# Last chunk's key-value products joined in held PSUM banks, two residuals added on TensorE, six spare matmuls taken out, and a new order table

## The chip, the cores and the metric

The kernel runs on one core of one Trainium2 chip. The metric is the device time of one execution, in microseconds (us); lower is better. A core has TensorE (PE, with its weight loads PEld), VectorE (DVE), ScalarE (ACT), GpSimd (POOL) and SyncE (SP), which here only issues DMAs. PSUM is used as four double banks of 128 x 1024 float32 (the program's D0 to D3, "D" in the profile).

## The reference

Two attention layers A and two linear layers B alternate on x of 2048 tokens by 512, bfloat16, 32 heads of 16. Cut to what matters here:

```python
x = A_x
x = x + _A_ref(_layernorm(x), A_wq, A_wk, A_wv, A_wo, A_beta)
x = x + _B_ref(_layernorm(x), B_wqkv, B_w_phi, B_wo)
x = x + _A_ref(_layernorm(x), ...)
x = x + _B_ref(_layernorm(x), ...)

# _B_ref
phi_k = concatenate([softmax(pk), softmax(-pk)], -1)      # pk = k @ w_phi, per head
kv = einsum('bhsf,bhsd->bhfd', phi_k, v)                  # sum over all 2048 tokens
z = einsum('bhsf->bhf', phi_k)
num = einsum('bhqf,bhfd->bhqd', phi_q, kv)
den = einsum('bhqf,bhf->bhq', phi_q, z)[..., None] + 1e-06
return (num / den) ... @ wo
```

Layer A works on four segments of 512 tokens: causal attention inside the segment, plus a read from a memory that the earlier segments have filled. Layer B needs its kv and z over all tokens before the first query can be answered, so every B layer has one turning point: the end of the keys.

## The kernel before

The sixteen tiles of 128 tokens are held in SBUF as `X`. A small graph (`Graph.op`) records every operation with what it reads and writes; `Graph.place` (L172) then takes three things from a compressed table, `ORDER`: the sequence of all operations, the engine of each, and the buffer of each tile. `Graph.emit` (L205) writes one instruction stream per engine in that sequence and puts semaphore waits where an engine needs another's result or a buffer that another still uses. Each engine runs its stream strictly in the table's order, and SP its DMAs too. No planner runs in the kernel: where the table puts an operation is where it runs.

The helpers name most lines of the profile. `mm` (L334, matmuls at L341) and `pair` (L345, matmuls at L356) issue matmuls on 64 rows of the array, so that two run side by side; `pair` issues two halves, and its second half waits for its first (`hard=o1`). `act` is L366, `evac` copies out of PSUM at L374 (ACT) or L375 (DVE), `tr` is a DMA transpose from SP (L383), `dma` a plain one (L387).

For each segment s of a layer: the A attention of its four tiles (`a_att`, in two halves), the output projection `out_proj` (L905), whose result is added to `X` by DVE (`res`, L926), the layer norm (L590 to L619), and the B keys of the chunk (`b_keys`, L950). Tiles 14 and 15 are projected one at a time (`SOLO`), the others in pairs. `b_keys` makes, for the tiles of a "part", the key projection (BK), two exponentials on ACT, their sums on DVE (`Zred`, L985), reciprocals (`rZ`, L405), the value projection (BV), its scaling by the reciprocals (`Vt`, L1007), and then the key-value products (KV): for each of two groups q of the feature blocks, one `pair` into a double bank of its own, which `kv_add` (L930) adds into `KV32` in SBUF (`KVacc`, L937 for the first, L939 for the others). Chunks 0 to 2 are one part of four tiles; chunk 3 is two parts, `((0, 1, 2), (3,))`: three tiles, then the last tile alone. After the last of them come the masked copies `Rkv` (L943) and `Rz` (L946), which the queries read.

`b_query` (L1029) makes the query projections (BQ) and their exponentials on ACT, the denominators on PE (`Zq`, L1049, from `Rz`) with a chain of small ACT and DVE steps after them (L1058 to L1068), then for each tile the numerators (`N`, L1076, from `Rkv`), a product (`nmul`, L1087 or L1090), the sum of two halves (`nadd`, L1093, on DVE or POOL by the table), a DMA transpose (`otr`), the projection, the add into `X` and, in the second layer, the store.

At the end of the program `keep` (L671) adds six pairs of 64 x 512 matmuls on a constant, whose result nobody reads; the table puts them in the last 35 us.

## Time and profile before

| | |
|---|---|
| median of 3 runs | 463.37 us (462.33 to 463.4) |
| the profiled execution | 462.93 us, of which 461.2 us are the span from the first to the last instruction |
| mean granted TensorE clock | 0.998 |
| busy share of the span | PE 95%, ACT 91%, DVE 90%, POOL 17% |

One execution was profiled. The rows name the line of the helper, the engine, the operation and its operands by the program's names. Matmuls overlap, so the start of one row to the start of the next tells more than the length of a row: eight 64 x 512 matmuls read as 1.04 us, and the next row begins 0.87 us after they did.

### The profile page before, as it was taken

What the parts mean: (1) busy time and instruction counts of PE and PEld (TensorE: products, weight loads), DVE (VectorE), ACT (ScalarE), POOL (GpSimd) and SP (SyncE); (2) the same over time, 40 slices, a digit from 0 to 9 for tenths busy, and PEclk for the clock granted to TensorE, in tenths of its full rate; (3) what the DMA queues carried; (4) which work ended last, traced back from release to release, by engine and by line L of the source; (5) the groups of instructions that cost most, each with busy time, mean ns of one, the idle gap of its engine ahead of it and who ended that gap; (6) DMA issues with size and microseconds to landing.
All of it is one profiled execution on the core that took longest, in us unless ns stands there. A gap on an engine that the chain in (4) does not pass through costs nothing.

```text
span 461.2 us, 25354 instructions
## 1 busy us (share of the span) xinstructions
PE 437.7 (95%) x11716; PEld 295.6 (64%) x11716; DVE 416.2 (90%) x807; ACT 420.3 (91%) x542; POOL 80.1 (17%) x160
## 2 busy tenths in 40 slices
PE   8989899899999999998899999999999999998896
PEld 4456667667776776675456677677677677666553
DVE  6989998898889999898999899998899889998896
ACT  4999999899999998789699999999999999878991
POOL 2402021101221211102532031130221023110020
PEclk9999999999999999999999999999999999999999
DMA  8554642552233322100243443264113321200357
GB/s 247 127 150 80 127 63 37 75 96 54 50 46 54 46 40 36 37 3 4 48 54 78 71 85 72 49 96 61 26 39 49 50 39 27 48 14 1 50 121 180
DMA packets 90058, 30.37 MB, mean 66 GB/s; under 512 B 76640, under 2 KB 89952, under 8 KB 89952
## 3 DMA queue, kind: packets, MB, share of 16 engines
q1 hardware_dynamic: 89520, 28.48, 33.3%
q8 instruction: 92, 1.51, 1.4%
q10 hardware_dynamic: 432, 0.27, 0.2%
q14 instruction: 14, 0.11, 0.1%
HBM read 6.32 MB, written 2.10 MB: 18 GB/s over the span
## 4 chain that ended last, share of the span: by engine, by line
PE 48%; ACT 40%; DVE 6%; DMA 3%; issue 2%; SPq 0%
PE D L356 31%; ACT p L366 21%; PE D L341 15%; ACT pF L366 13%; ACT pE L366 5%; DMA p<-p 2%; PE D L662 2%; DVE X L926 1%; DMA X<-in_A_x_dram 1%; DVE p L1090 1%; DVE p L375 1%; DVE stats L590 1%; ACT pS L366 1%; DVE p L611 0%; DVE pK L375 0%
## 5 line engine op out<-in xcount | busy, mean ns | idle before, releaser
L366 ACT ACTIVATE p<-D 128x1024 bf16<-128x1024 f32 (+2 forms) x224 | 216.0, 1004 | 13.5 <-PE D L356 9.7
L366 ACT ACTIVATE pF<-D 128x896 bf16<-128x896 f32 x128 | 116.7, 940 | 2.8 <-PE D L341 2.5
L341 PE MATMUL D<-pK,pQ 64*128 64x256 bf16 (+3 forms) x1536 | 112.9, 243 | 4.1 <-ACT pF L366 1.0
L341 PEld LDWEIGHTS D<-pK,pQ 64*128 64x128 bf16 x1536 | 55.2, 94 | 40.7 <-ACT pF L366 5.4
L341 PE MATMUL D<-pV,pF 64*128 64x34 bf16 x1024 | 73.8, 175 | 0.4 <-ACT p L366 0.4
L341 PE MATMUL D<-pW,pF 64*128 64x34 bf16 x1024 | 71.3, 175 | 0.0
L341 PEld LDWEIGHTS D<-pV,pF 64*128 64x128 bf16 x1024 | 55.3, 93 | 2.3 <-ACT p L366 0.7
L341 PE MATMUL D<-pV,p 64*128 64x34 bf16 x1024 | 53.3, 176 | 0.3 <-issue 0.2
L366 ACT ACTIVATE pE<-D 128x768 bf16<-128x768 f32 x64 | 52.3, 831 | 1.4 <-PE D L341 1.0
L341 PEld LDWEIGHTS D<-pW,pF 64*128 64x128 bf16 x1024 | 51.9, 93 | 0.9
L341 PE MATMUL D<-pW,p 64*128 64x34 bf16 x1024 | 52.1, 176 | 0.0
L598 POOL TENSOR_SCALAR rstd<-mv 128x1 f32<-128x1 f32 x60 | 16.1, 272 | 205.9 <-DVE mv L591 205.5
L341 PEld LDWEIGHTS D<-pV,p 64*128 64x128 bf16 x1024 | 47.0, 93 | 3.3 <-issue 0.9
L341 PE MATMUL D<-tri,two 64*128 64x128 bf16 (+1 forms) x384 | 46.7, 234 | 0.4 <-issue 0.4
L341 PEld LDWEIGHTS D<-pW,p 64*128 64x128 bf16 x1024 | 45.2, 93 | 1.3
L590 DVE BATCH_NORM_STATS2 stats<-X 128x6 f32<-128x512 bf16 x64 | 42.9, 680 | 3.0 <-DMA X<-in_A_x_dram 2.5
L341 PE MATMUL D<-pV,pE 64*128 64x34 bf16 x512 | 44.9, 175 | 0.4 <-issue 0.4
L926 DVE TENSOR_TENSOR X<-X,D 128x1024 bf16<-128x1024 bf16 (+1 forms) x36 | 39.4, 1095 | 5.7 <-PE D L356 5.0
L341 PE MATMUL D<-pW,pE 64*128 64x34 bf16 x512 | 42.5, 175 | 0.1
L985 DVE TENSOR_REDUCE pS<-p 128x64 f32<-128x1024 bf16 (+1 forms) x36 | 38.8, 1088 | 1.8 <-ACT p L366 1.8
L375 DVE CAST p<-D 128x512 bf16<-128x512 f32 x48 | 31.1, 683 | 6.3 <-PE D L356 6.1
L356 PE MATMUL D<-WB_o,p 64*128 64x512 bf16 (+1 forms) x288 | 33.0, 353 | 2.7 <-issue 1.3
(115 smaller groups left out, 988.9 us busy)
## 6 DMA issues: line engine op xcount, KB each, us to landing
pW<-pV SPq DMA_DIRECT2D x16, 136.0 KB, 3.1
out_dram<-X SPq DMA_DIRECT2D x7, 256.0 KB, 2.8
X<-in_A_x_dram SPq DMA_DIRECT2D x3, 512.0 KB, 6.1
pX<-in_B_wqkv_dram SPq DMA_DIRECT2D x3, 512.0 KB, 4.6
p<-p SPq DMA_TRANSPOSE x76, 2.8
pX<-p SPq DMA_TRANSPOSE x54, 3.2
WA_k<-in_A_wk_dram SPq DMA_DIRECT2D x2, 256.0 KB, 6.3
WA_q<-in_A_wq_dram SPq DMA_DIRECT2D x2, 256.0 KB, 7.0
```

The source lines that it names most:

```text
L341: ins = e.matmul(out_ap, lhsT, rhs, start=st, stop=sp, tile_position=(basep(lhsT), basep(out_ap)))
L356: ins = e.matmul(out_ap, lhsT[64 * hf:64 * hf + 64], rhs[64 * hf:64 * hf + 64], start=k == 0 and i == 0, stop=k == 1 and i == len(lists[hf ...
L366: return self.g.op({"act": (dur, lambda e: e.activation(out_ap(), in_ap(), func, scale=scale))}, reads, writes, opens, label=label)
L375: "dve": ((340 if fast else n / 0.96 + 65), lambda e: e.tensor_copy(out_ap(), in_ap()))}
L590: v(lambda e: e.bn_stats(self.stats[:, t, :], self.X[:, t, :]), 602, [R("X", t)], [R("st", t)], label="bn")
L598: v(lambda e: e.tensor_scalar(rs, self.mv[:, t, 1:2], LN_EPS, None, op0=ALU.add), 170, [R("mv", t)], [R("rstd", t)], eng="pool", label="rstd")
L662: ins = e.matmul(D.t[c0:, r0 * 8:r0 * 8 + n], r[:, c0:], ones(r, n), start=True, stop=True, tile_position=(r0, c0))
L926: self.v(lambda e: e.tensor_tensor(X(), X(), src(), ALU.add), 65 + 512 * n / 0.96, pr + xr, xr, label="res")
L985: fn = lambda e, sgn=sgn, eo=eo, Z=Z, n=n: e.tensor_reduce(Z.t[:, 0:64 * n].rearrange("p (k s h) -> p k s h", k=n, s=2)[:, :, sgn, :], eo( ...
L1090: v(lambda e, N=N, Tm=Tm, w=w, shape=shape: e.tensor_tensor(shape(Tm.t[:]), shape(N.t[:]), w(), ALU.mult), 1131, [N, AB[(0, 0)], AB[(0, 1) ...
```

## The change

Five things, cut from the diff:

```diff
-    def pair(self, items, cols, reads, writes, opens=(), label="", swap=False):
+    def pair(self, items, cols, reads, writes, opens=(), label="", swap=False, begin=True, end=True, prev=None):
...
-    ... start=k == 0 and i == 0, stop=k == 1 and i == len(lists[hf]) - 1,
+    ... start=begin and k == 0 and i == 0, stop=end and k == 1 and i == len(lists[hf]) - 1,
...
-        o1 = self.g.op({"pe": (dur, half(0))}, reads, writes, opens, label=label, rows=64)
+        o1 = self.g.op({"pe": (dur, half(0))}, reads, writes, opens, label=label, rows=64, hard=prev)
...
             for q in range(2):
-                ps = self.T(self.pD, "gen")
-                self.pair(...
+                join = (L, c) in JOIN
+                if not join or part[0] == 0:
+                    held[q] = (self.T(self.pD, "gen"), None)
+                ps, prev = held[q]
+                o2 = self.pair(...
-                    [ps[0]], label="KV")
-                self.kv_add(ps, q, c == 0 and part[0] == 0, c == 3 and part[-1] == 3)
+                    [ps[0]], label="KV", begin=not join or part[0] == 0, end=not join or part[-1] == 3, prev=prev)
+                held[q] = (ps, o2)
+                if not join or part[-1] == 3:
+                    self.kv_add(ps, q, c == 0 and part[0] == 0, c == 3 and part[-1] == 3)
...
-        res_pe = kind == "b" and all((L, t) in RES_PE for t in ts)
+        res_pe = all((kind, L, t) in RES_PE for t in ts)
...
-RES_PE = set()
+RES_PE = {('a', 1, t) for t in range(14, 16)}
+JOIN = {(0, 3), (1, 3)}
+RZ_ACT = set()
...
-        for _ in range(N_KEEP):
-            self.keep()
...
-N_KEEP = 6
```

1. **Join.** In chunk 3 of both layers the products of the last tile go on adding into the double banks that hold the products of the first three; one add into `KV32` per group takes the place of two. Four `KVacc` go, two in each layer. The first matmuls of the last tile wait for the end of the first part's second half in the same bank (`prev`).
2. **Residual.** For tiles 14 and 15 of the second A layer `X` is added by PE: one more block of matmuls, identity times `X`, in the accumulation (`extra` in `tproj`), and the result is then only copied out of PSUM into `X`.
3. **Keep.** The six pairs of matmuls are gone.
4. **A path not taken.** With `RZ_ACT` the reciprocals could be made on ACT; the set is empty, so nothing changes.
5. **New table.** It holds 2738 operations in place of 2748 (four adds and six `keep` fewer). Read operation by operation in the same way as `place` reads it, and compared with the old one: on PE an operation stands 1.0 places from where it stood on average (at most 11), on ACT 0.3, on DVE 5.1, on SP 3.8. 26 operations change engine. The two residual copies go to ACT. Of the sums `nadd` four go from DVE to POOL and one comes back in the first layer's queries, and in the second layer that of tile 4 goes from POOL to DVE; of the sums after the attention (L882) four go to POOL and four come back; the rest are copies out of PSUM that change places between ACT and DVE, one more leaving ACT than coming to it apart from the residuals, and one small fill of a buffer.

Around the turning point of the second layer PE's stream reads as follows (a "2" is the second half; KV16 to KV19 are the pairs of the first part, groups 0 and 1, then those of the last tile; BQ half-pairs are eight 64 x 512 matmuls each):

```text
before: KV16 KV17 KV16-2 KV17-2 BQ8-2 | KV19 BQ12 KV18 KV19-2 BQ12-2 KV18-2 | Zq17 Zq19 Zq18 Zq16
after:  KV16 KV17 KV16-2 KV17-2 BQ8-2 | KV19 KV18 BQ12 KV19-2 KV18-2 BQ12-2 | Zq27 Zq18 Zq17 Zq16
```

Before, the table gave KV19 the double bank of KV16 and KV18 that of KV17; both had to wait for the adds. At the end of SP's stream, the last DMA transpose (`otr` of tile 14) and a store change places. The buffer that this transpose writes is another one too: before, it was the one from which the transpose of tile 13 reads, so that it had to wait for that one to land; after, it is one that was last read by the projection of tiles 4 and 5. The order of the two:

```text
before: otr(tile 13) otr(tile 12) store(tiles 10, 11) otr(tile 14) store ...
after:  otr(tile 13) otr(tile 12) otr(tile 14) store(tiles 10, 11) store ...
```

## The prediction

> **What bounds the kernel now.** I read the page first, then the busy time by stages, then the chain of waits at the end, then the timeline around the edits.

> ```profile
> 100.00:150.00 50.00, 49.00 (x1449) 35.05 (x1446) 44.86 (x83) 49.93 (x61) 8.59 (x15) 1.00 0.29 51
> 150.00:186.00 36.00, 35.27 (x1118) 24.50 (x1115) 33.51 (x56) 33.62 (x44) 5.30 (x10) 1.00 0.29 41
> 250.00:384.00 134.00, 131.91 (x3951) 93.97 (x3945) 122.19 (x241) 132.65 (x164) 22.17 (x44) 1.00 0.34 56
> 384.00:425.00 41.00, 40.14 (x910) 27.60 (x905) 37.77 (x65) 34.99 (x43) 6.95 (x12) 1.00 0.13 25
> 400.00:412.00 12.00, 12.00 (x184) 6.88 (x177) 11.63 (x20) 9.55 (x12) 1.64 (x4) 1.00 0.17 34
> 425.00:440.00 15.00, 12.72 (x428) 8.21 (x430) 13.35 (x33) 14.59 (x26) 0.00 (x0) 1.00 0.35 54
> ```

> Columns: length, then busy time of PE, PEld, DVE, ACT, POOL, the granted clock, DMA. Three regimes. In the attention (100 to 186, 250 to 384) ACT is full: of 220 us it is idle for 0.07 + 2.38 + 1.35 = 3.8. Towards the turning point of a B layer (384 to 425) PE is full and ACT has room. From 425 ACT is full again, until 440; after that the end hangs on DMAs, as the next view shows. All edits but the table lie in the last two regimes.

> ```profile
> 413.06 11.10 PE D L356 x188
> 424.18 0.73 DVE KV L939
> 424.94 0.21 DVE Rz L946
> 425.19 0.98 PE D L341 x64
> ...
> 434.22 0.39 PE D L678 x2
> ...
> 435.80 0.21 PE D L678 x2
> ...
> 453.12 3.71 DMA p<-p
> ...
> 458.21 0.69 DVE X L926
> ```

> This is the chain that ended last: PE's stream to 424.18, one add, one `Rz`, the first `Zq` at 425.19; later two of the spare pairs (L678); at the end one DMA transpose, 3.71 us, the last projection and the last add.

> **Join, second layer.**

> ```profile
> 420.89 1.34 DVE L939 TENSOR_TENSOR KV<-KV,D 128x544 f32<-128x544 f32 x2
> 421.66 0.22 PEld L356 LDWEIGHTS D<-pT,p 64*128 64x128 bf16 x4 [0.21 <-DVE KV L939]
> 421.98 4.60 ACT L366 ACTIVATE p<-D 128x1024 bf16<-128x1024 f32 x5 [0.20 <-PE D L356]
> 422.98 0.55 PEld L356 LDWEIGHTS D<-pX,WB_q 64*128 64x128 bf16 x8
> 423.20 0.72 DVE L939 TENSOR_TENSOR KV<-KV,D 128x544 f32<-128x544 f32 x1 [0.96 <-PE D L356]
> 423.64 0.32 PEld L356 LDWEIGHTS D<-pT,p 64*128 64x128 bf16 x4
> ```

> The adds that go are the two at 420.89, 1.34 us of DVE. They lie under PE's stream; of them only the 0.21 us is on the path that PE waited for the first add to free the bank. The adds of the last tile stay. The half BQ12-2 (422.98) moves behind KV18-2, which so comes 423.64 - 422.98 = 0.66 us earlier, while the other add still ends only some 0.72 us after its products. So the last add starts not at 424.18 but between 423.3 (all of 0.21 + 0.66 saved) and 423.7 (behind the other add), and `Zq` could start 0.4 to 0.9 earlier. But ACT counts too: it works without a gap on five exponentials from 421.98 to 426.58, and the last two need BQ12, which now ends last; it saves only the 0.21. The first `Zq` of the new order also serves another chunk (64 of them in 0.98, so 16 take 0.24). I take -0.3, between +0.3 and -0.9. The new wait (`prev`) is for KV16-2 and KV17-2; behind it stands all of PE, but BQ8-2's eight matmuls lie in between, so it costs nothing; without that cover it would be a stall of the 0.21 kind for each group.

> **Join, first layer.**

> ```profile
> 202.43 1.35 DVE L939 TENSOR_TENSOR KV<-KV,D 128x544 f32<-128x544 f32 x2
> 203.22 0.80 PEld L356 LDWEIGHTS D<-pT,p 64*128 64x128 bf16 x16
> 204.19 1.35 DVE L939 TENSOR_TENSOR KV<-KV,D 128x544 f32<-128x544 f32 x2 [0.41 <-PE D L356]
> ```

> Here PE did not wait for the first adds (the second row has no idle time before it), and DVE itself waited 0.41 for PE before the last ones. Removing 1.35 under cover gives nothing; the new order puts one BQ half between the last two KV halves, which lets the first add start earlier and the second later. -0.2, between +0.3 and -0.4.

> [...] Here the table gave KV16 and KV19, and KV17 and KV18, the same double bank before, so the holding takes no bank that was free, and the sum has no term for it.

> **Residual.**

> ```profile
> 186.03 1.92 PE L356 MATMUL D<-WA_o,p 64*128 64x256 bf16 x32
> 406.60 0.68 DVE L926 TENSOR_TENSOR X<-X,D 128x512 bf16<-128x512 bf16 x1
> L374 ACT ACTIVATE p<-D 128x512 bf16<-128x512 f32 x28 | 15.9, 597 | 6.7 <-PE D L356 4.6 <-PE D L341 1.9
> ```

> The first row is the same pair of projections in the first layer: 32 matmuls in 1.92, so the eight added ones cost 0.48 of PE, in the stage (400 to 412) where PE is full 12.00 of 12. They take 2 x 0.68 from DVE, which is full too (11.63), and give ACT 2 x 0.60 by the nearest row, where it has 2.45 free. PE sets the end of this stage, so I take +0.4; bounds 0.5 (all of PE's) and -0.5 (the layer norm of these tiles, which waits for the result, comes earlier by part of DVE's 1.36).

> **Sums moved to POOL.**

> ```profile
> 225.00:237.00 12.00, 10.74 (x180) 5.42 (x180) 11.90 (x23) 9.19 (x17) 4.27 (x7) 1.00 0.17 35
> 237.00:250.00 13.00, 13.00 (x223) 7.76 (x223) 12.83 (x28) 12.95 (x18) 3.30 (x8) 1.00 0.60 95
> L1093 POOL TENSOR_TENSOR p<-p 128x512 bf16<-128x512 bf16 x10 | 12.3, 1231 | 65.1 <-DVE p L1090 33.2 <-DVE p L1087 31.6 <-DVE nb L605 0.2
> L1093 DVE TENSOR_TENSOR p<-p 128x512 bf16<-128x512 bf16 x16 | 6.8, 422 | 0.1
> ```

> Three net `nadd` leave DVE, 3 x 0.42 = 1.27 us. Up to 237 DVE alone is full, after it all three are: I take half, -0.6. Each moved sum is 0.81 later (1231 - 422 ns) at its transpose, so the bounds are -1.3 and +0.8. The four sums each way after the attention cancel, as do the copies, within ACT's 0.6.

> **Keep.**

> ```profile
> 447.33 0.59 PE L678 MATMUL D<-onesb 64*128 64x512 bf16 x4
> 447.54 2.85 ACT L366 ACTIVATE p<-D 128x1024 bf16<-128x1024 f32 x3 [0.38 <-PE D L341]
> ```

> Two pairs stand in front of the numerators for which ACT waits 0.38; two others are 0.39 + 0.21 of the chain above, but in a stage where ACT is full 14.59 of 15. I take -0.4, bounds 0 and -1.0.

> **The last transpose.**

> ```profile
> 450.86 1.20 SPq L383 DMA_TRANSPOSE p<-p  x1
> 451.17 0.42 DVE L1093 TENSOR_TENSOR p<-p 128x512 bf16<-128x512 bf16 x1
> 452.10 0.58 SPq L387 DMA_DIRECT2D out_dram<-X  x1
> 453.12 1.19 SPq L383 DMA_TRANSPOSE p<-p  x1
> 456.39 1.22 DVE L926 TENSOR_TENSOR X<-X,D 128x1024 bf16<-128x1024 bf16 x1 [0.17 <-PE D L356]
> ```

> Tile 14's sum ends at 451.59, SP is free at 452.06, yet its transpose starts at 453.12, behind a store and with its buffer not yet free. In the new table it is ahead of that store and in another buffer: 1.06 earlier. The store moved behind loses nothing that lasts: stores end the program only after the last add. DVE's add before the last one ends at 457.61, 0.60 before the last starts, so -0.6 is sure to have room and the rest needs DVE to be earlier too, which the two terms above give. -1.0, bounds 0 and -1.5.

> Sum: -0.3 - 0.2 + 0.4 - 0.6 - 0.4 - 1.0 = -2.1. The profiled execution is 462.93, 1.73 more than its span; the median is 0.44 above it, inside the spread of the three runs. Less 2.1 they give 460.8 and 461.3; I take the shift from the median, **461.3**. The terms' bounds, not all at one end, make its own range 460.0 to 462.8.

> **Rivals.** *The joins and the tail are covered (463.1).* PE and ACT are full before and after 425; if only the residual's +0.4 and the spare pairs' -0.4 reach the end and the transpose gains 0.3, nothing measurable is left. For it: DVE's saved adds are not on the chain. Against: the chain's end shows the gap at SP.

> *The new order closes gaps in the attention (459.2).* Of ACT's idle 3.8 us there 2.38 lie in one stage of 36; were that as tight as the other 184, which lose 1.42, it would lose 0.28, and 2.1 would go on top of the forecast's 2.1. PE's stream is only slightly changed, which speaks against much.

> *The new order opens gaps (466).* The place is the attention, where every exponential that starts late is lost time: if a products' block moves ahead of the scores that ACT needs next, ACT waits. The worst stage now loses 2.38 of 36 (6.6%); the other 184 us lose 1.42. At half the worst rate everywhere, 220 x 0.033 = 7.3, which is +3.5 and, with half of the gains, +2.5. It decides the sign once ACT's idle time there grows by more than the 2.1 gained elsewhere, and can be told from no change at 2.1 + 1.4. For it: DVE's order moves 5.1 places on average; against: ACT's 0.3.

> *The clock falls without the spare pairs (466.6).*

> ```profile
> 447.00:459.00 12.00, 9.26 (x152) 4.86 (x146) 10.44 (x15) 3.61 (x5) 0.00 (x0) 1.00 0.67 153
> 459.00:461.20 2.20, 0.00 (x0) 0.00 (x0) 0.00 (x0) 0.00 (x0) 0.00 (x0) 0.63 0.55 190
> ```

> The granted clock is full to 459 and falls as soon as PE has stopped. If PE's gaps, now filled, made it fall to half from 447 on, PE's 9.26 us of work would double and its 2.74 of idle time swallow a part: +6.5; over half of the stretch +3.3. With the middle, 4.9, and the other terms' -1.7 the time would be 466.6. [...]

> **How the numbers follow.** Forecast 0.50, covered 0.17, gaps closed 0.14, gaps opened 0.14, clock 0.05. From no change I can tell 0.3%, 1.4 us: faster is below 461.98, slower above 464.76. The forecast gives 0.40 of its 0.50 to faster, since most of its own range lies below 461.98, and gaps closed all of its 0.14: 0.54. Same: the other 0.10, covered 0.17, and 0.02 of gaps opened: 0.29. Slower: 0.12 + 0.05 = 0.17. The range, 458.2 to 465.2, leaves out the far parts of both order cases and most of the clock's, about 0.04 + 0.09 + 0.04.

> **What would show it.** Right: the first `Zq` of the second layer within 0.5 of 425.2; four adds fewer at L939; PE not waiting there for an add; the last transpose starting within 0.2 us of SP's previous one, and the last add about 1 us after the add before it starts; DVE below full before 237. Wrong: any ACT idle time in the attention off 3.8 by over 1.5, a granted clock under 1 before the last matmul, or a longer PE stretch than 0.5 before 424.

## The result, and the profile after

The changed kernel is slower: 467.53 us median of 4 runs (466.72 to 471.48) against 462.85 of the kernel before beside it, a ratio of 1.0125 (95% interval 1.0094 to 1.0156). On another chip, measured again (the run after_again below), it was 1.0172 (1.0132 to 1.0213). The forecast was 461.3, its range 458.2 to 465.2. One of the twelve executions of the run no_keep below took 1447.48 us; its median does not hang on it.

The busy time by stages of the changed kernel, with the columns of the prediction's first view:

```profile
100.00:150.00 50.00, 49.31 (x1448) 34.91 (x1440) 44.93 (x83) 49.92 (x62) 9.20 (x15) 1.00 0.34 58
150.00:186.00 36.00, 35.03 (x1090) 24.94 (x1086) 33.06 (x56) 33.18 (x43) 3.19 (x8) 1.00 0.25 34
225.00:237.00 12.00, 12.00 (x166) 5.88 (x166) 11.84 (x21) 9.32 (x15) 6.13 (x8) 1.00 0.19 38
237.00:250.00 13.00, 13.00 (x307) 8.50 (x305) 12.84 (x27) 12.90 (x18) 4.68 (x8) 1.00 0.46 74
250.00:384.00 134.00, 129.77 (x3808) 90.63 (x3804) 116.76 (x230) 129.47 (x158) 23.63 (x44) 0.99 0.36 55
400.00:412.00 12.00, 12.00 (x242) 7.78 (x238) 11.55 (x22) 8.48 (x11) 2.83 (x5) 1.00 0.25 36
425.00:440.00 15.00, 12.53 (x372) 7.80 (x368) 11.61 (x28) 13.45 (x23) 0.00 (x0) 0.77 0.26 38
```

In the attention ACT is now idle for 0.08 + 2.82 + 4.53 = 7.43 us, against 3.8. Nearly all of the growth lies between 250 and 384, where before it was 1.35; PE loses too (129.77 busy, before 131.91). And the granted clock is under 1 in two stages in which it had been 1.00.

The same view cut at the places where the clock changed, first of the changed kernel, then of the kernel before around its turning point:

```profile
314.82:318.23 3.41, 2.56 (x159) 2.38 (x152) 2.86 (x6) 2.71 (x5) 0.00 (x0) 1.00 0.40 70
318.23:321.65 3.42, 3.42 (x25) 1.30 (x22) 1.52 (x2) 2.65 (x3) 0.00 (x0) 0.50 1.10 105
427.46:430.87 3.41, 2.69 (x176) 2.37 (x168) 1.53 (x4) 3.35 (x9) 0.00 (x0) 1.00 0.02 5
430.87:437.70 6.83, 5.85 (x132) 3.65 (x134) 6.61 (x17) 5.86 (x11) 0.00 (x0) 0.50 0.39 61
```

```profile
425.44:428.86 3.42, 2.83 (x186) 2.52 (x179) 1.81 (x5) 3.33 (x9) 0.00 (x0) 1.00 0.02 5
428.86:432.27 3.41, 2.94 (x110) 1.94 (x111) 3.41 (x10) 3.41 (x8) 0.00 (x0) 1.00 0.15 31
```

The clock is halved for one stretch of 3.41 us in the attention and for two of them after 430.87, each time after a stretch in which PE was busy for 2.56 and 2.69 of 3.41 us. It was far from idle there.

The rows of PE's timeline of the changed kernel that begin after idle time with no releaser (the bracket has the idle time and what ended it; "issue" means that PE waited for nothing that the profile shows):

```profile
280.35 0.19 PE L341 MATMUL D<-pV,pF 64*128 64x34 bf16 x1 [0.88 <-issue]
284.37 0.19 PE L341 MATMUL D<-pW,pF 64*128 64x34 bf16 x1 [0.56 <-issue]
300.41 0.19 PE L341 MATMUL D<-pV,p 64*128 64x34 bf16 x1 [0.39 <-issue]
317.25 0.41 PE L341 MATMUL D<-MSb,p 64*128 64x4 bf16 x19 [0.70 <-issue]
431.55 0.23 PE L341 MATMUL D<-Rz,p 64*128 64x24 bf16 x4 [0.99 <-issue]
```

Four of them, 2.53 us, lie in the second attention; the fourth and the fifth stand inside one operation of the graph, which has no semaphore to wait for in its middle.

The end of the chain of waits after, and DVE's timeline there:

```profile
453.07 1.22 DVE p L1087 x2
454.29 2.60 DMA p<-p
456.94 1.05 PE D L356 x8
458.04 1.06 PE D L356 x8
459.12 1.22 DVE X L915
```

```profile
459.12 1.22 DVE L915 TENSOR_TENSOR X<-X,D 128x1024 bf16<-128x1024 bf16 x1 [1.00 <-PE D L356]
460.26 0.16 DVE L521 CAST H8b<-H 128x8 bf16<-128x8 f32 x1
460.33 1.28 DVE L915 TENSOR_TENSOR X<-X,D 128x512 bf16<-128x512 bf16 x2
```

The last transpose is off the chain, as it should be. In its place stands the transpose before it (454.29), whose two-tile projection and its add of 1.22 come last on PE's and DVE's way, and the two single adds queue behind that add. (Lines of the changed file have moved: `res` is L915 there instead of L926, the adds of `kv_add` L928 instead of L939, `Rz` L935 instead of L946.)

Where the time went, stage by stage, for this and for the runs below: the start of the same ACT instruction in two traces, minus its start in the trace of before, median over a stretch of instructions, and then the change of that from one stretch to the next. The last column is the span's difference to 461.2. A plus is time lost.

```text
                      to 250  250-335  335-390  390-417  417-427  427-446  446-end   span
after                  -2.41    +4.25    +0.01    +0.46    -0.05    +0.61    +0.44  +3.31
after_again            -0.44    +3.92     0.00    +0.46    -0.05    +0.67    +0.92  +5.48
keep_back              +0.11    +3.88    -0.01    +0.46    -0.05    +0.67    -0.06  +5.00
o_early                -0.25    -0.13    +0.32    +0.46    -0.05    +0.80    +0.85  +2.00
o_early_keep           -0.63    +1.93    +0.02    +0.46    -0.05    +0.93     0.00  +2.66
o_early_dve_res        -0.60    +2.31    +0.02    +1.37    +0.39    +0.64    +0.81  +4.94
no_keep                -2.65    +0.42    -0.45     0.00     0.00    +0.35    +3.14  +0.81
old_order_edits        +0.69    +0.15    -0.12    +2.11     0.00    +0.24    -0.56  +2.51
old_order_edits_keep   +0.05    -0.14    +0.20    +2.11     0.00    +0.41    -0.14  +2.49
join_only              -0.09    -0.05    +0.03     0.00     0.00    +0.38    +0.06  +0.33
o_late                 -0.83    +1.18    -0.09    +0.01    -0.01    +0.53    +0.20  +0.99
tail_only              -1.87    +0.03    -0.07     0.00     0.00    +0.07    +0.28  -1.56
pe32_new               -1.58    +2.27    -0.50    +0.01     0.00    +0.36    +0.02  +0.58
pe32_back              -0.36    +4.09    +0.04    +0.46    -0.05    +1.34    -0.07  +5.46
pe32_back_o_early      +1.18    +4.64    +0.06    +0.46    -0.05    -0.09    +0.16  +6.36
```

The first column is mostly scatter: before, no_keep, o_late, tail_only and pe32_new run the same instructions up to 250, and stand there at 0, -2.65, -0.83, -1.87 and -1.58. Most of it arises before 100 us. From 390 to 427 the columns repeat to a few hundredths wherever two kernels are alike. Between 250 and 390 alike kernels differ by up to 0.5 (no_keep, +0.42 and -0.45, behind a stall of 0.36 at 314.39), and the last column holds more than the work, as the section on the end shows. For differences of 1 us and more this is still a finer instrument than the times. The largest entry of the changed kernel is the second attention, and 4.25 is what the four stalls (2.53) and one stretch of half clock (at most 3.41 / 2 = 1.71) make together, by estimate: 4.24.

### The profile page after: what moved, and what is told of

Read it like the earlier page. It is cut to its first block, busy times and chain, and to the rows that moved or that the text cites. A ratio compares the mean times of both kernels' runs of the same rounds, so it can differ in the third digit from the quotient of the medians.

```text
span 464.5 us, 25334 instructions
## 1 busy us (share of the span) xinstructions
PE 440.1 (95%) x11712; PEld 297.3 (64%) x11712; DVE 411.8 (89%) x799; ACT 420.0 (90%) x543; POOL 83.6 (18%) x163
## 4 chain that ended last, share of the span: by engine, by line
PE 53%; ACT 36%; DVE 5%; DMA 3%; issue 2%; DVEq 0%; ACTq 0%; SPq 0%
PE D L356 35%; ACT p L366 19%; PE D L341 18%; ACT pF L366 10%; ACT pE L366 4%; DMA beta_sb<-in_A_beta_dram 2%; DMA p<-p 1%; DVE stats L590 1%; DVE p L1087 1%; DMA X<-in_A_x_dram 1%; DVE p L375 1%; DVE X L915 1%; ACT p L608 1%; ACT pS L366 1%; DVE p L1090 0%
## 5 line engine op out<-in xcount | busy, mean ns | idle before, releaser
L366 ACT ACTIVATE p<-D 128x1024 bf16<-128x1024 f32 (+2 forms) x224 | 215.1, 1004 | 15.4 <-PE D L356 11.8
L366 ACT ACTIVATE pF<-D 128x896 bf16<-128x896 f32 x128 | 116.5, 939 | 3.5 <-PE D L341 3.1
L341 PE MATMUL D<-pK,pQ 64*128 64x256 bf16 (+3 forms) x1536 | 113.7, 243 | 2.9 <-ACT pF L366 0.6
L341 PEld LDWEIGHTS D<-pK,pQ 64*128 64x128 bf16 x1536 | 55.3, 94 | 38.7 <-ACT p L366 4.9
L341 PE MATMUL D<-pV,pF 64*128 64x34 bf16 x1024 | 74.0, 175 | 1.3 <-issue 0.9
L341 PE MATMUL D<-pW,pF 64*128 64x34 bf16 x1024 | 71.7, 175 | 0.6 <-issue 0.6
L341 PEld LDWEIGHTS D<-pV,pF 64*128 64x128 bf16 x1024 | 55.4, 93 | 3.3 <-issue 1.3
L598 POOL TENSOR_SCALAR rstd<-mv 128x1 f32<-128x1 f32 x60 | 17.1, 298 | 214.8 <-DVE mv L591 213.8
L341 PE MATMUL D<-pV,p 64*128 64x34 bf16 x1024 | 53.2, 176 | 0.6 <-issue 0.6
L366 ACT ACTIVATE pE<-D 128x768 bf16<-128x768 f32 x64 | 52.5, 834 | 1.1 <-PE D L341 0.5
L341 PEld LDWEIGHTS D<-pW,pF 64*128 64x128 bf16 x1024 | 52.0, 93 | 1.8 <-issue 0.7
L341 PE MATMUL D<-pW,p 64*128 64x34 bf16 x1024 | 52.2, 176 | 0.3 <-issue 0.3
L341 PEld LDWEIGHTS D<-pV,p 64*128 64x128 bf16 x1024 | 47.1, 93 | 2.7 <-issue 0.5
L341 PEld LDWEIGHTS D<-pW,p 64*128 64x128 bf16 x1024 | 45.6, 93 | 1.8 <-issue 0.4
L341 PE MATMUL D<-tri,two 64*128 64x128 bf16 (+1 forms) x384 | 46.6, 234 | 0.0
L915 DVE TENSOR_TENSOR X<-X,D 128x1024 bf16<-128x1024 bf16 (+1 forms) x34 | 37.9, 1121 | 7.9 <-PE D L356 7.5
L341 PE MATMUL D<-pV,pE 64*128 64x34 bf16 x512 | 44.6, 175 | 0.0
L341 PE MATMUL D<-pW,pE 64*128 64x34 bf16 x512 | 42.7, 175 | 0.0
L375 DVE CAST p<-D 128x512 bf16<-128x512 f32 x49 | 32.1, 681 | 6.2 <-PE D L356 5.7
L600 POOL TENSOR_TENSOR rstd<-rstd,mhalf 128x1 f32<-128x1 f32 x60 | 35.8, 600 | 3.7
```

Source lines behind the costliest of these rows:

```text
L341: ins = e.matmul(out_ap, lhsT, rhs, start=st, stop=sp, tile_position=(basep(lhsT), basep(out_ap)))
L366: return self.g.op({"act": (dur, lambda e: e.activation(out_ap(), in_ap(), func, scale=scale))}, reads, writes, opens, label=label)
L375: "dve": ((340 if fast else n / 0.96 + 65), lambda e: e.tensor_copy(out_ap(), in_ap()))}
L598: v(lambda e: e.tensor_scalar(rs, self.mv[:, t, 1:2], LN_EPS, None, op0=ALU.add), 170, [R("mv", t)], [R("rstd", t)], eng="pool", label="rstd")
L600: v(lambda e: e.tensor_tensor(rs, rs, self.mhalf[:], ALU.pow), 540, [R("rstd", t), R("mhalf")], [R("rstd", t)], eng="pool", label="rstd")
L915: self.v(lambda e: e.tensor_tensor(X(), X(), src(), ALU.add), 65 + 512 * n / 0.96, pr + xr, xr, label="res")
```

## The experiments

Each group of runs was timed beside the kernel before on the same chip; ratios are to that.

| run | median us | before | ratio (95%) |
|---|---|---|---|
| keep_back | 467.68 | 461.15 | 1.0124 (1.0098 to 1.0151) |
| no_keep | 462.81 | 461.15 | 1.0029 (1.0007 to 1.0050) |
| old_order_edits | 464.35 | 461.15 | 1.0063 (1.0041 to 1.0085) |
| old_order_edits_keep | 464.42 | 461.15 | 1.0066 (1.0046 to 1.0087) |
| pe_order_back | 481.64 | 460.84 | 1.0472 (1.0428 to 1.0515) |
| o_early | 465.66 | 460.84 | 1.0111 (1.0084 to 1.0137) |
| join_only | 462.13 | 460.84 | 1.0031 (1.0019 to 1.0043) |
| new_then_old | 472.33 | 460.84 | 1.0252 (1.0231 to 1.0273) |
| o_late | 463.82 | 462.65 | 1.0018 (0.9992 to 1.0043) |
| tail_only | 462.72 | 462.65 | 1.0003 (0.9981 to 1.0024) |
| o_early_keep | 467.36 | 462.65 | 1.0118 (1.0076 to 1.0160) |
| o_early_dve_res | 469.57 | 462.65 | 1.0161 (1.0122 to 1.0201) |
| after_again | 469.58 | 461.18 | 1.0172 (1.0132 to 1.0213) |
| pe32_back | 470.75 | 461.18 | 1.0205 (1.0158 to 1.0252) |
| pe32_back_o_early | 469.36 | 461.18 | 1.0176 (1.0135 to 1.0217) |
| pe32_new | 463.77 | 461.18 | 1.0052 (1.0031 to 1.0073) |

### The spare pairs

keep_back puts the six pairs into the new order; no_keep takes them out of the old one.

```diff
 N_WARM = 16
+N_KEEP = 6
 PE: Zq26 Zq25
+    keep0
 PE: N19 Zq23 N26 N16
+    keep3
 PE: ... otp4
+    keep4
 PE: ... Wo27-2
+    keep2
 PE: ... N28
+    keep5 keep1
```

> The changed kernel with its six spare pairs put back into PE's order near their old neighbours (four between the second `Zq` block and the last query projection, two ahead of the last numerators). Theory "clock": the second fall of the granted clock (430.9 to 437.7) comes from PE's thin stream of 24- and 64-column matmuls without the pairs; with them the clock is 1.00 from 425 to 455 and the time falls by 0.6 to 1.5 us below the changed kernel, to 466.0-466.9; the stretch 285 to 325 stays as it is. Rival "order": the loss is all in the new table's attention; the time stays within 0.4 of 467.5 and the eight projections at 434-438 take the same time whatever the clock. Rival "pairs cost": as the prediction had it, each pair is PE time on the path, so +0.4.

```diff
-N_KEEP = 6
+N_KEEP = 0
```

> The kernel before without its six spare pairs, nothing else. Theory "clock": the granted clock falls to half once or twice between 425 and 440 and the time rises by 0.6 to 1.5 us, to 463.5-464.4. The prediction's term: the pairs stand in front of the numerators, so 0 to 1.0 us faster, 461.9-462.9, with the clock at 1.00.

no_keep is slower, by 0.3 to 2.3 us, and its profile shows where. The stages of no_keep, cut at its clock's changes:

```profile
424.85:431.68 6.83, 6.14 (x166) 4.03 (x160) 5.73 (x15) 6.83 (x14) 0.00 (x0) 0.50 0.20 41
431.68:448.74 17.06, 14.13 (x332) 7.69 (x327) 15.89 (x31) 15.19 (x21) 2.42 (x2) 1.00 0.58 103
448.74:452.15 3.41, 3.38 (x31) 1.66 (x33) 1.63 (x3) 0.60 (x1) 0.00 (x0) 0.50 0.62 154
```

The first fall, two stretches long, costs only 0.35 in the end (table, 427 to 446): ACT is full there, 6.83 of 6.83. From 446 to its end the kernel loses 3.14, and the second fall explains a part of that alone. Up to the end of the last add the loss is 1.29; in it, eight matmuls at 448.77 take 1.89 us at half clock, where before they took 1.04. The other 1.84 lie behind the last add, which ends at 457.86, ahead of the 458.90 of before: from there the program needs another 4.15 us, before 2.31, in which no engine computes and the last stores land. So the time without the pairs is longer by 1.7 us (0.3 to 2.3), about what theory "clock" expected, but the clock is shown as the cause of a part only. old_order_edits below has no pairs either, and its clock is full from 436.96 to the end.

In the new order the medians show no gain from the pairs (1.0124 with, 1.0125 and 1.0172 without; keep_back stands as far above before as the changed kernel does, as rival "order" said). The columns from 427 on add up to 0.61 and 0.93 with the pairs and to 0.07 to 1.65 without, but of the latter 0.6 to 1.2 lie behind the last add. The clock falls after 430 with the pairs too, so theory "clock" does not explain the loss.

### The edits under the old order

```diff
 ORDER = the table of before, without the removed operations
-res of tiles 14, 15: DVE
+res of tiles 14, 15: ACT
```

> The changed code (joined KV groups, residual of tiles 14 and 15 by PE with ACT emptying the bank, no spare pairs) under the table of before, with only the removed operations taken out. Theory "order": the attention is as before (ACT idle 1.3 to 1.6 us between 250 and 384, clock 1.00 there), and the time is that of the kernel before, -0.1 for joins and residual, plus what the missing pairs cost: 463-464.5. Rival "edits": the joins or the residual are what costs; then the time is 466 or more.

> As the run above, with the six spare pairs where the kernel before had them. Theory "order": joins -0.5 and residual +0.4 leave 462.0-463.4, with the clock at 1.00 until PE has ended. Rival "edits": 465 or more. The difference to the run above is the price of the missing pairs: theory "clock" 0.6 to 1.5, the prediction's term -1.0 to 0.

```diff
-RES_PE = {('a', 1, t) for t in range(14, 16)}
+RES_PE = set()
 JOIN = {(0, 3), (1, 3)}
 N_KEEP = 6, ORDER = the table of before without the four adds
```

> The kernel before with nothing but the join: both layers' last KV groups add into held banks, its own table less the four adds; residual by DVE, spare pairs in place. From the step that the run old_order_edits_keep shows at 204 us (0.87 later behind a wait of 0.70 for an add) and none at 425: +0.9 against before, 461.6-462.6. The prediction's terms: -0.5, 460.2-461.1.

All three leave the attention as it was (+0.15, -0.14 and -0.05), so the 4 us there belong to the table. By the times the edits without the new table cost 0.6%, with it 1.2 to 1.7%. But the edits are not free either. Both old-order runs are 3.2 to 3.3 us above the kernel before beside them, more than theory "order" allowed and as much as rival "edits" asked for (its 466 and 465 stand 3.2 and 2.2 above the 462.85 of before known then), though not in the attention. Under the old order the residual costs 2.11 between 390 and 417. ACT's timeline of old_order_edits_keep shows why:

```profile
406.71 0.60 ACT L374 ACTIVATE X<-D 128x512 bf16<-128x512 f32 x1 [0.82 <-PE D L356]
408.66 0.60 ACT L374 ACTIVATE X<-D 128x512 bf16<-128x512 f32 x1 [1.36 <-PE D L356]
```

The copies stand in ACT's queue where DVE's adds stood in the table, and the exponentials behind them wait 0.82 and 1.36 for PE. And join_only is 0.3% slower. PE's timeline of it has one row that the kernel before lacks:

```profile
203.72 2.14 PE L356 MATMUL D<-pX,WB_q 64*128 64x512 bf16 x16 [0.70 <-DVE KV L939]
```

The query projection that took over the first group's bank, emptied early before, now waits for the add at the very end. ACT's instructions step back by 0.88 there (from -1.19 at 199 us to -0.31 at 208), and nothing comes back at the second join (417 to 427: 0.00). The spare pairs make no difference that the times show (1.0063 and 1.0066).

### Two splices that tell nothing of their own

```diff
 PE, first to last exponential of the second layer (351 operations):
-the new order
+the order of before
```

> The changed kernel with PE's order in the attention of the second layer (351 operations between the first and the last of its exponentials) taken from the table of before; the other engines keep the new order but for 18 operations that must give way by up to five places, and 35 buffers change number. Theory "supply": in the new order short matmuls follow each other so closely that PE runs out of instructions (idle 0.88, 0.55, 0.38, 0.69 us with no semaphore to wait for, between 280 and 318), and one stretch of half clock follows; with the old order these four are gone, the clock is 1.00 there, and the time falls by 2.5 to 4.2 us, to 463.3-465.0. Rival "queue": what is lost there hangs on SP's late transposes; then the time stays within 1.0 of 467.6.

```diff
 ORDER up to the first exponential of the second layer: new
-                                   from there on: new
+                                   from there on: before, with joins and pairs
```

> The new table up to the first exponential of the second layer, the table of before from there on, with both joins and the spare pairs, without the residual by PE. If the loss lies in the new table's second attention: no stall there, and the time is that of before, less what the new start gains (0 to 2.4 in the two profiles): 459.0-461.5. If it lies ahead of it: 464 or more.

Both came out far worse than either parent. PE and ACT then disagree on the order of their work, and some 35 tiles had to take other buffers: in new_then_old PE waits 4.55 us at one place for an exponential. They suggest that order and buffers belong together, and show nothing of the question.

### The queue of DMA transposes

```diff
 SP: PhKtr PhKtr
+    otr(first o tile of the 266 us projection)
 SP: otr otr otr PhKtr
-    otr(first o tile of the 266 us projection)
 SP: otr
```

> The changed kernel with one DMA transpose (the first o tile of the second layer's 265 us projection, in the new table the seventh of its batch on SP, before the first) moved four places up on SP; six buffers change number, nothing else moves. Theory "queue": PE's wait of 2.04 us for that transpose, seen in one profile at 266, is gone in all runs, and the median falls by 0.5 to 2 us, to 465.6-467.1. Theory "supply": PE still runs out of instructions later on, and the median stays at 467-468.

```diff
 SP (table of before):
-    otr(the same tile)
 SP: otr otr PhKtr PhKtr otr
+    otr(the same tile)
 SP: PhKtr PhKtr PhKtr PhKtr
```

> The kernel before with one DMA transpose moved on SP: the first o tile of the projection at 266 us goes from first to sixth of its batch, behind two of the others, two phi transposes and one more o tile (two PE operations next to each other change places with it). Theory "queue": it is then issued at about 260 instead of 251 and its projection waits for it in a part of the runs: median 0.3 to 2.0 us above before, with a wait of PE for a DMA of p at 266. Rival: the ten us of lead were never needed, median within 0.3 of before (461.0).

> The changed kernel unchanged, beside the next three. Theory "supply": PE again stands still without a semaphore at some of the same four places between 280 and 318 (counted in its instructions: 14274, 14530, 15298, 16322), 0.5 to 2.5 us in all; 1.2% above before.

after_again is the changed kernel unchanged. PE's timeline, ACT's, the stages and SP's timeline of that execution:

```profile
267.66 1.04 PE L356 MATMUL D<-WB_o,p 64*128 64x512 bf16 x8 [2.11 <-DMA p<-p]
```

```profile
268.97 1.02 ACT L366 ACTIVATE p<-D 128x1024 bf16<-128x1024 f32 x1 [2.04 <-PE D L341]
271.23 0.81 ACT L366 ACTIVATE pE<-D 128x768 bf16<-128x768 f32 x1 [1.24 <-PE D L341]
```

```profile
265.37:268.78 3.41, 1.30 (x20) 0.53 (x16) 1.58 (x6) 1.55 (x2) 0.00 (x0) 1.00 0.41 72
268.78:272.19 3.41, 3.41 (x34) 1.86 (x32) 1.22 (x1) 1.83 (x2) 0.00 (x0) 0.50 0.56 112
```

```profile
253.71 13.25 SPq L383 DMA_TRANSPOSE p<-p  x8
```

In the table of before that tile's transpose is the first of the batch, issued at 251.08; in the new one it is the seventh, issued at 261.11 in the first profile and at 263.54 here, at the end of thirteen us of transposes back to back. PE wants it at 265.55. It waits 2.11 us, the clock halves, and 3.92 are lost. The first profile of the changed kernel was lucky at this place (its projection began 0.11 after the matmul ahead of it) and lost as much through stalls later. keep_back waited 2.04 here, pe32_back only 0.28: two of the four profiles with the transpose in seventh place show the long wait, none of the four with it in third place. The issue alone does not decide it: from issue to landing the transpose took 4.1 and 4.0 us in the two with the wait, 2.5 in the other two. o_early's profile loses nothing in this attention (-0.13), but two others with the early transpose lose 1.9 and 2.3 to stalls, a third (pe32_back_o_early) 4.64, most of it for another reason (below), and the ratios overlap. So the wait is shown, and no profile with the transpose moved up has it; what it is worth in the median is not shown. o_late doesn't decide it: PE waits for no DMA there. Of its step of 1.18 some 0.95 arise at 266, where the two PE operations changed places (0.62 of waiting for an exponential), and the rest behind a stall of 0.47 with no semaphore at 285.64.

### The end, and what is left in the new order

```diff
 SP:  otr(tile 13) otr(tile 12)
-     store(tiles 10, 11) otr(tile 14)
+     otr(tile 14, another buffer) store(tiles 10, 11)
 PE:  Wo29
+     Wo29-2
 PE:  Wo30 otp5
-     Wo29-2
```

> The kernel before with nothing but the end of the queue as in the new table: the last DMA transpose ahead of the store it stood behind and into the buffer that the projection ahead of it frees, for which that projection's second half runs two places earlier on PE; spare pairs, adds and residual as before. The prediction's term: 0.6 to 1.0 us faster than before, 460.0-460.4 against 461.0. Theory of the trace of the changed kernel: the add of the two-tile projection follows right behind and takes 0.4 of it away, so 0.2 to 0.6 faster. Rival: nothing, within 0.2.

The transpose starts 0.88 after its sum instead of 1.53, and nothing comes of it: 1.0003. The end of tail_only's chain of waits:

```profile
449.75 0.88 DVE X L926
450.63 4.31 DMA p<-p
```

Before, the DMA read 3.71. Issued 0.65 earlier in relation to the sums, it takes 0.60 longer, so the last add starts where it did (the sum's end to the start of the last add: 6.57 now, 6.62 before).

What lies behind the last add changes as well. In the profile of before the last store is issued at 458.92, 1.28 after the store ahead of it, and the program ends 2.29 later. In tail_only the two stores are 0.87 apart and the end comes 2.60 after the last, in the changed kernel 0.60 and 2.86, in no_keep 0.60 and 4.12. In all 18 profiles it is 2.2 to 2.3 where the last store stood 1.28 or more behind the one ahead of it, and 2.6 to 4.1 where it stood 0.5 to 0.9 behind. Of the last column of the table 0.58 lie behind the last add in the changed kernel, where the column has +0.44, and 1.16 in after_again, where it has +0.92: up to that add both gain a little. That the closeness of the stores is the cause was not tested.

> The run o_early with the six spare pairs put back as in keep_back. Theory "clock": with the second attention free of the wait, the tail's half clock is what is left, and the pairs take away one or both of its windows: 464.4-465.4 against o_early's 465.7. Rival: pairs do not help in the new order, 465.7 or more.

```diff
-RES_PE = {('a', 1, t) for t in range(14, 16)}
+RES_PE = set()
-res of tiles 14, 15: ACT
+res of tiles 14, 15: DVE
```

> The run o_early with the residual of tiles 14 and 15 on DVE again, in the same order otherwise: eight matmuls less on PE and two additions of 0.68 on DVE in place of two copies of 0.60 on ACT. The prediction's term and the step seen between 394 and 411 in o_early's profile (+0.5): 0.4 to 0.5 faster, 465.2. Rival: the new order was made for ACT's copies and DVE, full there, loses 0.5 or more: 466.2.

In the new order the residual on DVE costs 1.37 + 0.39 between 390 and 427 where PE's matmuls and ACT's copies cost 0.46 - 0.05: the edit is right for the order it came with and wrong (2.11) for the other. In both runs the rival came true: o_early_keep (1.0118) is no faster than o_early (1.0111), and o_early_dve_res (1.0161) is slower, though the intervals overlap; the columns show the step more sharply.

### PE's own order

```diff
 PE, 32 operations around 278 to 288 us:
-new order (pe32_back, pe32_back_o_early); order of before (pe32_new)
+order of before;                          new order
```

> The changed kernel with 32 consecutive PE operations (around 278 to 288) in the order of before; nine DVE operations give way by up to five places, no buffer changes. If PE's own order makes it run out of instructions: no stall over 0.3 at 14274 and 14530, and 0.5 to 1.4 faster than after_again. If not: the two stalls stay and the time is within 0.5.

> The same 32 operations put back, in o_early. Theory "queue" and "supply" together: 1.5 to 3 us faster than after_again, 464.5-466 if that is 467.5; what is left is the tail and the residual. If only the transpose mattered: 0.5 to 2 faster.

> The kernel before with those 32 PE operations in the new order (one bank and four ACT operations change place). If PE's own order is the cause: stalls of 0.3 to 0.9 at 14274 and 14530 and 0.5 to 1.4 slower than before. If not: none, and within 0.5 of before.

The stalls do not go with these operations alone. pe32_back has none at 14274 and 14530 but two further on (0.40 and 0.71), pe32_back_o_early three (0.45, 0.76 at 14274, and 0.74), and pe32_new none of 0.3 in that attention; it loses 2.27 there because its PE and ACT now take exponentials in different orders. The other two lose 2.7 and 3.8 at the exchanged operations, pe32_back by waits for exponentials too, so their times answer neither question. In all, the eight profiles of kernels with the new attention show 18 stalls of 0.3 us or more between 250 and 335, the eight with the old attention three (no_keep 0.36, o_late 0.47, tail_only 0.34; the splices left aside). So they are more frequent with the new order, and up to 0.88 long, but not new. Which of the moved operations lets PE run into them is open.

## Why the prediction was wrong

**The step that failed** is the weighing of the table. The prediction costed each edit where it stood and gave the attention no term, and the rival "opens gaps" 0.14, against which it set ACT's 0.3 places (and, against the rival "closes gaps", a stream of PE that is "only slightly changed"). In place of nothing the second attention cost 4.25 us in the first profile, by four stalls of PE without a semaphore and a stretch of half clock, and 3.92 in the second, by a wait of 2.11 for one transpose and a stretch of half clock. Under the old order the same edits leave it unchanged (at most 0.15). The rival named the right place and the right sign: ACT's idle time grew by 3.6, well past its 2.1. Its mechanism, a block of products ahead of the scores, is not what these two profiles show, so that its 466 and the clock rival's 466.6 lie so near to 467.53 is in part luck. The means of places moved said nothing: SP's 3.8 were in the list, and among them was one transpose that lost ten us of lead. Following each transpose of the batch to the PE operation that waits for it would have found this one; which moves bring the stalls stays open.

**The clock rival** was given 0.05 for two errors. It looked only from 447 on, and it took PE's idle time as the measure, which no run shows. The clock fell in the attention and at the turning point, with PE busy for some three quarters of the stretch before. It was not the lone cause it was thought to be: in the attention stalls of 0.4 to 0.9 us or the wait of 2.1 stand ahead of its fall, which then adds up to 1.71 (half of a stretch) to what they cost.

**Keep**, -0.4: wrong in sign for the kernel before, which is 0.3 to 2.3 us slower without the pairs; with the edits or the new order the times show no effect (1.0063 and 1.0066, 1.0124 and 1.0125). Two pairs ahead of the numerators were read as an obstacle for ACT (0.38). In no_keep's profile the clock falls where they are missing, but 1.84 of the 3.14 lost there come after the last add, so the cause is shown only in part.

**Last transpose**, -1.0: measured 0 alone. That it started too late was right; that its DMA would land as much earlier was not (4.31 against 3.71). In the changed kernel it does start within 0.1 of SP being free, as forecast, and the two-tile projection takes over the chain. The step that "stores end the program only after the last add" was right in words, but it took the time behind that add as fixed, and it grew from 2.31 to 2.89.

**Sums to POOL**, -0.6: 0. DVE is full to 250 as before (11.84 of 12, 12.84 of 13), and ACT's instructions keep their distance to before from 224 to 247 (-0.41 and -0.41 in after_again). No run moves these sums alone.

**Joins**, -0.2 and -0.3: about +0.3 in the first layer (after_again steps from -0.73 at 201 to -0.41 at 224; ACT's own order changes there, so a few tenths are uncertain) and -0.05 in the second. The four adds are gone (12 at this line of `kv_add` in place of 16) and PE no longer waits for one, but the removed DVE time had been under cover, and the first `Zq` at 427.14 is late by what the attention lost.

**Residual**, +0.4: the stage shows +0.46, the one term that came out, but as the sum of the edit and the order. The edit alone cost 2.11 under the old order, because ACT's copies stand ahead of exponentials, and saved 1.35 under the new one. The reasoning (PE is full, 12.00 of 12, and eight matmuls cost 0.48) has neither number in it, so the agreement is luck.

Together, on the changed kernel's own trace: -2.7 of scatter ahead of the first join, +0.3 join, 0 sums, +4.25 attention, +0.46 residual, -0.05 join, +0.61 and +0.44 to the end, which is +3.3. No version tried here beats the kernel before.

## What to carry to other kernels

When a table of order changes, don't average the moves: for every DMA that moved on its queue, compare the time from its issue to the operation that needs it, and distrust a lead that shrinks as here, from 14.8 us (issued at 251.08, projection at 265.88) to 2.0 (263.54 and 265.55 in after_again). That finds the waits of this kind only; the stalls without a semaphore show in a profile alone. An edit and the order it was tuned with go together, so measure it in both; here the residual cost 2.1 in one and saved 1.3 in the other. On a full PE a stall can cost more than its length: here stalls of 2.53 us, and in another execution a wait of 2.11, were followed by a stretch of half clock, and 4.25 and 3.92 were lost. And look at what lies behind the last add before a loss at the end is put down to the work.

## What the hardware showed

**The clock.** The two falls ahead of the end of the changed kernel's program lie on one grid: from 318.23 to 430.87 is 112.64 us, 33.0 times 3.413, the length of the half-speed stretch at 318.23. Every half-speed stretch ahead of a program's end lasts one or two of these (3.41 and 6.83 in the changed kernel, 6.83 and 3.41 in no_keep). One passage can lie on it in more than one way: tail_only runs the turning point of before unchanged, 1.90 us earlier (first `Zq` at 423.29 against 425.19), and its clock falls there, at 425.03 (mean 0.996 of 459.6 us, the share of one such stretch), where that of before stays at 1.00. PE was not idle ahead of the falls shown above: of the 3.41 us before them it was busy for 2.56 and 2.69 in the changed kernel, for 1.30 in after_again. Counting the columns that the matmuls ending in a window (3.413 us on the grid) stream (columns times rows / 128), over the 18 profiled executions, from 8 to 456 us, at full clock:

```text
columns in a 3.413 us window   windows   followed by half clock
under 2800                          14                       14
2800 to 3240                        18                        7
3240 to 3850                        36                        0
```

The width of what PE streams parts the two kinds far better than its busy time, though not sharply. 176 matmuls of 24 and 64 columns in 2.69 busy us (3072 columns) were followed by half clock; before, 186 in the same passage (425.44 to 428.86), one spare pair of 512 columns among them, made 3960 and kept it. Without the pair it would be 3448, still in the last row. And no_keep kept the clock after only 1.95 busy us, with 3584 columns:

```profile
206.40:209.81 3.41, 1.95 (x56) 1.00 (x53) 2.65 (x7) 3.38 (x9) 0.00 (x0) 1.00 0.00 0
```
